# A fused mLSTM and two mixture-of-experts layers: the first w_in conversion placed behind the first score products, and a last routing with a split position

## The chip, the cores and the metric

One core of a Trainium2 chip runs the kernel. The metric is the device time of one execution in microseconds (us); lower is better. Times of instructions come from one profiled execution of the kernel before, counted from its first instruction.

## The reference

```python
# 1. mLSTM: batch 2, 8 heads, 768 steps, head width 40
m_new = max(f[t] + m, i[t]); C = exp(f[t]+m-m_new) * C + exp(i[t]-m_new) * outer(v[t], k[t])   # n likewise with k[t]
y[t] = sigmoid(o[t]) * (C @ q[t]) / max(abs(n @ q[t]), 1)
# 2. x: 1536 tokens x 320
g = softplus(x @ w_in);  x = g @ w_out                       # inner width 2048
# 3. 8 experts, each token goes to one
e = argmax(x @ w_gate)
out = softmax(x @ w_gate)[e] * sigmoid(x @ w_output_gate)[e] * (relu(x @ w1[e]) @ w2[e])   # inner width 1024
```

## The kernel before, in words

The mLSTM runs in chunks of 128 steps (NCH = 6) for two batches b. For each chunk and batch the gates are scanned (`gates`), a mask and the decays are made (`mask`, `decay`, ScalarE exponentials), the scores `sp` are multiplied on TensorE for the two halves hh of the heads and weighted by the decays on VectorE (`scores`; the result replaces the decays in tile `abc`), `pv` multiplies them with the values, and the result x goes to the first feed-forward layer. Chunk c of both batches is block c of 256 tokens.

Precision is kept by splitting every fp32 operand into a rounded fp32r part and its rest, so that products are made in several passes. `conv` (line 796) does that for the 16 pieces n of w_in and w_out, which arrive as 64-bit numbers: three VectorE operations each turn the two words into fp32 (`to_f32`, tiles `wra` and `wta`), a copy rounds, and two subtractions, on VectorE (`low`) and GpSimd (`low_p`), make the rest. The raw buffers are three; the load of the fourth piece on the SP queue waits until the first is read. `up1` and `down1` are the products `ph` and `acc` of this layer, for all blocks.

After the last f of a block, `route` finds each token's expert and its place in the expert's slots of 128 rows, and GpSimd scatters the rows to DRAM. For the last block `place_last` (line 1054) does the placing: from the counts per expert (`tot`), the rank of a token among those of its expert (`rank`), the room left in the expert's open slot (`room`), its next free row (`nxt`) and the new slots opened (scan `cum`), with `base` the correction for tokens that go to a new slot. The slots 0 to 3 don't wait for the scatter: `early_turn` transposes the rows that are in DRAM already (`er`) into `xe` and adds the last block's rows by products with a selection matrix `S` (1 where a row's place equals the column's number), for the rounded parts first and the rests (`parts_of`, `have_lows`) second; `early_x` splits `xe` into `flat` and its rest. Then `second` runs the experts in four quarters: `up` (`ph`), transposes `tp`, `down` (`yp`). Slots from 4 on load their rows (`yac`) after the scatter and transpose them as `xslot`.

The order on every engine is made by a planner on the host, the class `Weaver` (line 46). Tasks are generators; each says which events it waits for and on which engine its next operation goes. The planner keeps a modelled clock for each engine and gives the next place to the task that could start earliest; where two could start at the same time, the one with the lower rank goes first, and then the one added first. After an operation its task can't start the next dependent one on the same engine at once (0.13 us in the model), so others come in between. `W.op("P", cost)` adds modelled time on TensorE. On the chip each engine runs its list in order, and semaphores hold what isn't ready.

`warm(event, n)` puts n bf16 products of 512 columns, which nobody reads, on TensorE when `event` is marked. In the last routing: `known` is marked when the expert numbers of the first slots are read into TensorE's registers (`get_experts`), `have_turned` when the twelve transposes of `early_turn` are placed, `turned_rows[0]` when the first row group of the last block is transposed, and `have_last_lg` when its logits are done.

Of the kernel before, what the change touches and what calls it, by code (L numbers as in the profile page):

```python
# [14 lines left out]
ALU = mybir.AluOpType  # L15
# [219 lines left out]
def mlstm_moe_kernel(ctx: ExitStack, tc: tile.TileContext, q_t, k_t, k, v, i_gate, f_gate, o_gate,  # L235
# [142 lines left out]

    scored_1 = Event(n=2 * B - 1)
# [168 lines left out]
    def chunk(b, c):  # L548
# [65 lines left out]
        def scores(hh):  # L614
            yield [have_kt[b][c], have_q[c], masked[hh]]
            half = box["dd"][:, :, hh]
            sp, ev = yield from bank.get([P, NP, P], F32, "sp")
            for n in range(NP):
                if n % 2 == 0:
                    yield "P"  # L620
                PE.matmul(sp[:, n, :], kT[0:104, hh, n, :], qT[0:104, n, :], start=True, stop=True)
            W.signal(used_kt[b][c])
            W.signal(used_q[c])
            if c == 1:
                W.signal(scored_1)
            yield [decayed[hh]]
            yield "V"
            DVE.tensor_tensor(out=half, in0=sp, in1=half, op=ALU.mult)
            W.signal(ev)
            W.signal(scored[hh])  # L630
# [165 lines left out]
    def conv():  # L796
        for n in range(NF):
            W.cur.rank = RANKS[n]
            yield [have_raw[n]] + ([have_g[0]] if n == 0 else [])
# [72 lines left out]
    def tt(out_, a, b_, op):  # L872
        DVE.tensor_tensor(out=out_, in0=a, in1=b_, op=op)
# [180 lines left out]
    def place_last(small, tot, rank, ohb, ef, ssum, row, row_ev, ev, counts_ev, small_ev, blk, whole):  # L1054
# [5 lines left out]
        dn, t8, c1, c2 = (small[:, o9 + n * E:o9 + (n + 1) * E] for n in range(4))  # L1060
        own = small[:, 0:2]
# [4 lines left out]
        tt(m, rank, over(room, T2), ALU.is_ge)  # L1066
        yield "V"
        DVE.tensor_tensor_scan(out=cum, data0=newp, data1=more_p, initial=0.0, op0=ALU.add, op1=ALU.add)
        tt(nr, rank, over(nxt, T2), ALU.add)
        yield "V"  # L1070
        DVE.scalar_tensor_tensor(out=dn, in0=u, scalar=float(P), in1=base, op0=ALU.mult, op1=ALU.subtract)
        yield "V"
        tt(m, m, over(dn, T2), ALU.mult)
        yield "V"
        tt(nr, nr, m, ALU.add)
        yield "V"
        tt(nr, nr, ohb, ALU.mult)
# [3 lines left out]
        DVE.tensor_copy(out=posi, in_=pos)  # L1081
# [4 lines left out]
        for t in range(T2):  # L1086
            yield "V"
            DVE.tensor_scalar(out=chosen["S"][:, t], in0=chosen["iota"], scalar1=pos[:, t:t + 1], scalar2=None,
                              op0=ALU.is_equal)
# [375 lines left out]
    W.add(gates(1, 1, 2), 0.5)  # L1465
# [21 lines left out]
    def get_experts(s0, s1, ready, when):  # L1487
# [16 lines left out]
        W.op("P", 0.35 + 0.1 * (s1 - s0))  # L1504
# [18 lines left out]
    W.add(warm(known, 3), 0)  # L1523
    W.add(warm(turned_rows[0], 2), 0)
    W.add(warm(have_last_lg, 2), 0)
# [295 lines left out]
```

## Time and profile before

| | |
|---|---|
| median of three runs | 428.53 us (427.74 to 428.86) |
| the profiled execution | 425.7 us, its span 423.9 us |
| busy in the span: TensorE, VectorE, ScalarE, GpSimd | 97%, 78%, 71%, 45% |
| mean granted TensorE clock | 0.988 of full |
| data moved | 62.9 MB, mean 148 GB/s |

The span runs from the first to the last instruction; the execution's own time has 1.8 us more around it. Busy time of TensorE is modelled from the starts of its products, and a product that follows another closely is counted with its pipeline time. The idle time given in brackets behind a row is the time for which its engine had nothing to do before it, and behind the arrow stands what ended that. A row that says x12 stands for twelve instructions in a row, its second number is the time that they cover.

### The profile page before, as it was taken

The page shows a single profiled execution, that of the slowest core. Times are in us where ns is not written, and L with a number is a line of the kernel's source. Part 1 is how long each engine was busy: PE and PEld are TensorE (multiplying, and loading weights), DVE is VectorE, ACT ScalarE, POOL GpSimd, SP SyncE. Part 2 cuts the span into 40 slices and gives each one's busy share as a digit, 9 for nine tenths or more (in the row PEclk, how much of TensorE's full clock was granted, in tenths as well). Part 3 has the DMA queues.
Part 4 walks back from the last instruction along what each step waited for, and adds up shares of the span by engine and source line. Part 5 has one row for each costly group of instructions (what it writes and reads, how often), then busy time and mean ns, then how long its engine had stood idle before and what let it go on. Part 6 is the DMA issues. An engine that isn't in the chain of part 4 may idle for free.

```text
span 423.9 us, 9886 instructions
## 1 busy us (share of the span) xinstructions
PE 409.6 (97%) x3095; PEld 390.7 (92%) x3095; DVE 330.6 (78%) x900; ACT 301.2 (71%) x880; POOL 189.6 (45%) x256
## 2 busy tenths in 40 slices
PE   8898999999999999999999999989999999999994
PEld 7787999999989999999999999878999999999993
DVE  4997999889988999998765756756853686697863
ACT  3677999979767877876867877656788774675421
POOL 5265665656041102221210102127666867777765
PEclk9999999999999999999999999979999999999998
DMA  8959597581218982212100101128735836835022
GB/s 264 340 179 316 189 295 225 178 212 54 77 63 281 337 275 67 64 50 76 39 18 22 40 2 38 39 101 264 249 96 166 249 132 194 247 125 178 12 88 93
DMA packets 32283, 62.89 MB, mean 148 GB/s; under 512 B 4218, under 2 KB 16765, under 8 KB 32230
## 3 DMA queue, kind: packets, MB, share of 16 engines
q1 hardware_dynamic: 30742, 57.87, 43.6%
q0 software_dynamic: 1488, 4.35, 2.8%
q8 instruction: 28, 0.46, 0.4%
q14 instruction: 25, 0.20, 0.2%
HBM read 54.05 MB, written 8.65 MB: 148 GB/s over the span
## 4 chain that ended last, share of the span: by engine, by line
PE 87%; DVE 5%; ACT 3%; DMA 2%; POOL 1%; issue 1%; SPq 1%; POOLq 0%; ACTq 0%
PE ph L196 34%; PE acc L196 20%; PE yp L196 13%; PE pv L196 5%; PE sp L196 4%; PE tp L196 3%; PE lg L196 2%; DMA wra<-in_w_in_dram 2%; PE qc L196 2%; PE xe L196 1%; PE kv L196 1%; PE x2tp L196 1%; DVE wta L196 1%; PE xp L196 1%; SPq L196 1%
## 5 line engine op out<-in xcount | busy, mean ns | idle before, releaser
L196 ACT ACTIVATE ab<-ab 128x256 f32<-128x256 f32 x192 | 77.3, 415 | 2.6
L196 PE MATMUL ph<-w1s,flat 128*128 x312 | 60.9, 332 | 0.5 <-ACT flat L196 0.4
L196 POOL TENSOR_TENSOR w1s<-w1raw,w1s 64x256 fp32r<-64x256 f32 (+1 forms) x39 | 40.9, 1062 | 36.7 <-ACT w1s L196 16.2
L196 PE MATMUL acc<-win,gh 128*128 128x320 f32 x240 | 55.4, 316 | 0.4 <-ACT gh L196 0.4
L196 PE MATMUL yp<-w2s,hh 128*128 x240 | 54.6, 315 | 0.0
L196 PEld LDWEIGHTS ph<-w1s,flat 128*128 128x128 f32 x312 | 46.5, 189 | 5.0 <-ACT flat L196 0.6
L196 POOL TENSOR_TENSOR w2s<-w2raw,w2s 128x640 fp32r<-128x640 f32 x30 | 46.9, 1593 | 8.5 <-issue 5.0
L196 DVE SCALAR_TENSOR_TENSOR g<-ph,ab 128x256 f32<-128x256 f32 x96 | 40.0, 420 | 13.7 <-ACT ab L196 12.7
L196 ACT ACTIVATE ab<-ph 128x256 f32<-128x256 f32 x96 | 36.4, 379 | 18.0 <-PE ph L196 17.2
L196 DVE TENSOR_TENSOR gl<-g,gh 128x256 fp32r<-128x256 f32 x96 | 41.8, 442 | 8.5 <-ACT gh L196 7.9
L196 DVE TENSOR_TENSOR hr<-ph,hr 128x256 f32<-128x256 f32 x60 | 25.3, 424 | 27.2 <-ACT hr L196 27.0
L196 POOL DMA_INDIRECT rows<-row,rsm x12 | 12.5, 1044 | 75.1 <-DVE nxt L196 29.7
L196 ACT CAST gh<-g 128x256 fp32r<-128x256 f32 x94 | 37.3, 398 | 9.5 <-DVE g L196 9.0
L196 ACT COPY hr<-ph 128x256 f32<-128x256 f32 x60 | 23.0, 383 | 28.2 <-PE ph L196 28.2
L196 PE MATMUL ph<-win 128*128 128x256 f32 x250 | 41.4, 287 | 0.0
L196 PEld LDWEIGHTS yp<-w2s,hh 128*128 128x128 f32 x240 | 39.8, 188 | 1.5 <-issue 0.6
L196 PEld LDWEIGHTS acc<-win,gh 128*128 128x128 f32 x240 | 38.6, 189 | 1.0 <-ACT gh L196 0.9
L196 PE MATMUL yp<-w2s,hl 128*128 x120 | 37.2, 310 | 0.0
L196 PE MATMUL acc<-win,gl 128*128 128x320 f32 x120 | 37.2, 310 | 0.0
L196 PEld LDWEIGHTS ph<-win 128*128 128x128 f32 x250 | 34.5, 190 | 0.0
L196 PE MATMUL acc<-wou,gh 128*128 128x320 f32 x144 | 33.4, 316 | 0.0
L196 ACT CAST w2s<-w2raw 128x640 fp32r<-128x640 f32 x32 | 23.2, 745 | 14.0 <-PE yp L196 14.0
(211 smaller groups left out, 1065.5 us busy)
## 6 DMA issues: line engine op xcount, KB each, us to landing
w1raw<-in_w_dram SPq DMA_DIRECT2D x32, 384.0 KB, 3.1
wra<-in_w_in_dram SPq DMA_DIRECT2D x16, 704.0 KB, 6.9
w2raw<-in_w_dram SPq DMA_DIRECT2D x32, 320.0 KB, 3.4
abc<-abc_dram SPq DMA_DIRECT2D x4, 1024.0 KB
rows<-pad SPq DMA_DIRECT2D x19, 194.0 KB, 5.9
qT<-in_q_t_dram SPq DMA_DIRECT2D x6, 512.0 KB, 3.9
kn<-in_k_dram SPq DMA_DIRECT2D x5, 416.0 KB, 7.4
vn<-in_v_dram SPq DMA_DIRECT2D x6, 320.0 KB, 5.2
```

What stands on the lines that cost most here:

```text
L196: return fn(*args, **kw)
```

## The change

Four edits. `conv` waits, for its first piece, until two of the four weighted scores of chunk 0 are placed (event `scored_0`), instead of the first chunk's gates. The task of chunk 1's gates has rank 1.1 instead of 0.5, behind the conversion (rank 1 for the first four pieces). `place_last` computes the place of a token as two numbers, `pos` (row in the open slots, with the correction) and `new` (128 times the number of slots opened before the expert's), which are added for the scatter; the selection matrix subtracts the first and compares with the second in one operation. The planner counts reading the expert numbers with 0.1 us, where it counted 0.35 and 0.1 for each slot; the three warm-ups behind it wait for `have_turned`, those behind the first transposed rows are one instead of two, and those behind the last logits four instead of two.

```diff
+    scored_0 = Event(n=2)
     scored_1 = Event(n=2 * B - 1)
...
             W.signal(ev)
+            if c == 0:
+                W.signal(scored_0)
             W.signal(scored[hh])
...
-            yield [have_raw[n]] + ([have_g[0]] if n == 0 else [])
+            yield [have_raw[n]] + ([scored_0] if n == 0 else [])
...
-        dn, t8, c1, c2 = (small[:, o9 + n * E:o9 + (n + 1) * E] for n in range(4))
-        own = small[:, 0:2]
+        c1 = small[:, o9 + 2 * E:o9 + 3 * E]
+        own, new = small[:, 0:2], small[:, 3 * T2:4 * T2]
+        far = small[:, o8 + 2 * T8:o8 + 3 * T8].rearrange("p (t e) -> p t e", e=E)
...
         tt(m, rank, over(room, T2), ALU.is_ge)
+        tt(nr, rank, over(nxt, T2), ALU.add)
         yield "V"
         DVE.tensor_tensor_scan(out=cum, data0=newp, data1=more_p, initial=0.0, op0=ALU.add, op1=ALU.add)
-        tt(nr, rank, over(nxt, T2), ALU.add)
-        yield "V"
-        DVE.scalar_tensor_tensor(out=dn, in0=u, scalar=float(P), in1=base, op0=ALU.mult, op1=ALU.subtract)
-        yield "V"
-        tt(m, m, over(dn, T2), ALU.mult)
-        yield "V"
-        tt(nr, nr, m, ALU.add)
-        yield "V"
+        DVE.scalar_tensor_tensor(out=m, in0=m, scalar=float(P), in1=ohb, op0=ALU.mult, op1=ALU.mult)
         tt(nr, nr, ohb, ALU.mult)
         yield "V"
+        DVE.scalar_tensor_tensor(out=far, in0=m, scalar=1.0 / P, in1=over(base, T2), op0=ALU.mult, op1=ALU.mult)
+        tt(m, m, over(u, T2), ALU.mult)
+        yield "V"
+        tt(nr, nr, far, ALU.subtract)
+        DVE.tensor_reduce(out=new, in_=m, axis=AX.X, op=ALU.add)
+        yield "V"
         DVE.tensor_reduce(out=pos, in_=nr, axis=AX.X, op=ALU.add)
         yield "V"
-        DVE.tensor_copy(out=posi, in_=pos)
+        tt(posi, pos, new, ALU.add)
...
-            DVE.tensor_scalar(out=chosen["S"][:, t], in0=chosen["iota"], scalar1=pos[:, t:t + 1], scalar2=None,
-                              op0=ALU.is_equal)
+            DVE.tensor_scalar(out=chosen["S"][:, t], in0=chosen["iota"], scalar1=pos[:, t:t + 1],
+                              scalar2=new[:, t:t + 1], op0=ALU.subtract, op1=ALU.is_equal)
...
-    W.add(gates(1, 1, 2), 0.5)
+    W.add(gates(1, 1, 2), 1.1)
...
-        W.op("P", 0.35 + 0.1 * (s1 - s0))
+        W.op("P", 0.1)
...
-    W.add(warm(known, 3), 0)
-    W.add(warm(turned_rows[0], 2), 0)
-    W.add(warm(have_last_lg, 2), 0)
+    W.add(warm(have_turned, 3), 0)
+    W.add(warm(turned_rows[0], 1), 0)
+    W.add(warm(have_last_lg, 4), 0)
```

## Rows read from the trace of the kernel before

**Rows 1.** The page's 40 slices: the granted TensorE clock in tenths.

```profile
PEclk9999999999999999999999999979999999999998
```

**Rows 2.** Busy time of each engine by stage; first the stretch and its length.

```profile
13.80:36.00 22.20, 19.62 (x174) 17.91 (x175) 21.47 (x46) 15.06 (x54) 9.19 (x13) 1.00 0.80 247
36.00:45.00 9.00, 7.86 (x58) 6.20 (x57) 6.53 (x15) 7.75 (x23) 6.18 (x10) 1.00 1.02 326
45.00:275.30 230.30, 229.24 (x1831) 226.05 (x1830) 195.41 (x581) 181.69 (x563) 67.14 (x108) 1.00 0.38 118
...
288.45:417.60 129.15, 128.65 (x876) 120.86 (x873) 91.21 (x201) 82.28 (x197) 92.24 (x97) 1.00 0.53 168
```

**Rows 3.** Timeline of VectorE at the start: start, time covered, instructions, idle before.

```profile
11.80 1.04 DVE L196 TENSOR_SCALAR wta<-wra 128x704 uint32<-128x704 uint32 x1 [0.43 <-DMA wra<-in_w_in_dram]
...
13.70 1.27 DVE L196 TENSOR_TENSOR abc<-sp,abc 128x512 f32<-128x512 f32 x2
...
19.34 0.16 DVE L196 TENSOR_SCALAR gts<-gps 128x16 f32<-128x16 f32 x1
```

**Rows 4.** VectorE's busy time on tile scratch (chunk 1's gate split).

```profile
11.80:18.00 6.20, 1.36 (x5) 1.00 1.03 345
```

**Rows 5.** Timelines of ScalarE and TensorE at the start.

```profile
11.38 0.20 ACT L196 COPY sm<-abc 128x4 f32<-128x4 f32 x1
...
15.12 1.95 PE L196 MATMUL pv<-v,abc 128*128 128x123 f32 x16 [1.34 <-DVE abc L196]
```

**Rows 6.** Timelines of the SP queue and GpSimd: chunk 2's cumulated gates.

```profile
27.83 0.33 SPq L196 DMA_DIRECT2D abc_dram<-acum  x1
31.23 0.39 SPq L196 DMA_DIRECT2D abc<-abc_dram  x1
...
39.37 1.60 POOL L196 TENSOR_SCALAR_AFFINE_SELECT abc<-abc 128x512 f32<-128x512 f32 x2 [0.40 <-DMA abc<-abc_dram]
```

**Rows 7.** Timeline of TensorE around the last routing.

```profile
278.46 0.59 PE L196 MATMUL warm<-ones 128*128 128x512 bf16 x2
...
279.71 0.17 PE L196 MATMUL counts<-rsm,tri 128*128 128x8 bf16 x1 [0.66 <-DVE rsm L196]
...
279.84 2.24 PE L196 MATMUL xe<-ident,er 128*128 128x128 f32 x12
...
282.49 5.32 PE L196 MATMUL xe<-S,part 128*128 128x256 f32 x20 [0.42 <-DVE S L196]
...
287.66 0.82 PE L196 MATMUL warm<-ones 128*128 128x512 bf16 x3
...
288.45 4.00 PE L196 MATMUL ph<-w1s,flat 128*128 x24
```

**Rows 8.** Busy time in 1 us stretches; the third number from the end is the clock.

```profile
280.00:281.00 1.00, 1.00 (x8) 1.00 (x8) 0.95 (x10) 1.00 (x6) 0.00 (x0) 0.73 0.00 0
287.00:288.00 1.00, 1.00 (x7) 0.73 (x6) 0.76 (x3) 0.79 (x4) 1.00 (x2) 0.85 0.00 0
```

**Rows 9.** Timeline of VectorE in the last placing: first, third last, second last, selection.

```profile
280.02 0.17 DVE L196 TENSOR_TENSOR newp<-counts,room 128x8 f32<-128x8 f32 x1
...
281.59 0.17 DVE L196 TENSOR_REDUCE rsm<-rsm 128x2 f32<-128x16 f32 x1
...
281.79 0.17 DVE L196 CAST rsm<-rsm 128x2 uint32<-128x2 f32 x1
281.87 0.88 DVE L196 TENSOR_SCALAR S<-iota,rsm 128x512 fp32r<-128x512 f32 x2
```

**Rows 10.** Timeline of the other engines behind the selection.

```profile
280.55 3.85 ACT L196 CAST w2s<-w2raw 128x640 fp32r<-128x640 f32 x6
...
284.37 0.97 POOL L196 DMA_INDIRECT rows<-row,rsm  x1 [0.30 <-issue]
...
287.14 1.61 DVE L196 TENSOR_TENSOR flat<-xe,flat 128x256 fp32r<-128x256 f32 x4 [2.85 <-ACT flat L196]
287.29 2.35 SPq L196 DMA_DIRECT2D yac<-rows  x5
```

More of the change, by code (lines that the diff above doesn't have):

```diff
@@ L1066, in place_last @@
         tt(m, rank, over(room, T2), ALU.is_ge)
+        tt(nr, rank, over(nxt, T2), ALU.add)
         yield "V"
         DVE.tensor_tensor_scan(out=cum, data0=newp, data1=more_p, initial=0.0, op0=ALU.add, op1=ALU.add)
-        tt(nr, rank, over(nxt, T2), ALU.add)
+        DVE.scalar_tensor_tensor(out=m, in0=m, scalar=float(P), in1=ohb, op0=ALU.mult, op1=ALU.mult)
+        tt(nr, nr, ohb, ALU.mult)
         yield "V"
-        DVE.scalar_tensor_tensor(out=dn, in0=u, scalar=float(P), in1=base, op0=ALU.mult, op1=ALU.subtract)
+        DVE.scalar_tensor_tensor(out=far, in0=m, scalar=1.0 / P, in1=over(base, T2), op0=ALU.mult, op1=ALU.mult)
+        tt(m, m, over(u, T2), ALU.mult)
         yield "V"
-        tt(m, m, over(dn, T2), ALU.mult)
-        yield "V"
-        tt(nr, nr, m, ALU.add)
-        yield "V"
-        tt(nr, nr, ohb, ALU.mult)
+        tt(nr, nr, far, ALU.subtract)
+        DVE.tensor_reduce(out=new, in_=m, axis=AX.X, op=ALU.add)
         yield "V"
```

## The prediction, made before the result was known

> **What bounds the kernel now.** I read the page's slices first, then the busy time by stage, then timelines of the two stages that the diff touches. TensorE bounds most of it: from 45.0 to 275.3 us it is idle for only 1.06 of 230.3 us, and from 288.45 to 417.6 for 0.5 of 129 us [rows 2]. In between there is nearly nothing to win, and whatever brings TensorE's work forward at either end of these stretches is carried to the end of the span. The slack is in two places. At the start, TensorE is idle for 2.58 us between 13.8 and 36 and for 1.14 us between 36 and 45 [rows 2], while VectorE has 0.73 us of idle in the 22.2 us of the first of these stretches: VectorE is the engine that is late there. At the last routing the granted clock drops, the one 7 in the middle of the page's clock row [rows 1].
>
> All times below are of the profiled execution, 425.7 us with a span of 423.9. The three plain runs have a median of 428.53, 2.8 more; I work out differences in the profile and apply them to 428.53. A measurement tells 0.3%, 1.29 us, from no change.
>
> **Part 1, the start.** Before, VectorE stops for 0.43 us until the first w_in piece lands, runs that piece's first conversion step at 11.80 (1.04 us), a step of chunk 1's gates, and the second conversion step, and comes to chunk 0's first two score products only at 13.70 [rows 3]. What these need was there earlier: the last ScalarE step of both decays ends at 11.58 [rows 5]. TensorE waits 1.34 us for the second of them and starts pv at 15.12, so it was free at 13.78 [rows 5]. With the change no conversion can be placed ahead of the two products. They take 1.27 us [rows 3]; from 11.37 (the end of VectorE's work before its 0.43 us of waiting) they end at 12.64, or, if the five operations that split chunk 1's cumulated gates (1.36 in sum [rows 4]) all go first, at 14.0. Both are within 0.25 us of 13.78, so the wait of 1.34 us shrinks to 0 to 0.25.
>
> What of these 1.1 to 1.3 us lasts? VectorE's work up to 36 us is the same, only in another order, and it is full but for 0.73 us. So the lasting gain has VectorE's recovered idle time as its near bound, 0.4, and the whole TensorE wait as its far one, 1.3. The conversion itself ends later: three steps, put behind two products, end 0.4 to 1.3 us after where they did. Queued behind the third step are SP's next w_in load (it needs the raw buffer) and, behind that load on SP, chunk 1's second k, v and k-natural loads. DMA is at 80% of its engines over this stretch [rows 2], so those loads sit in a backlog anyway, and I cost the shift at nothing; without that backlog it would cost up to 1.3 us at chunk 1's v. Chunk 1's remaining gate steps yield to the conversion where both are ready; that loss is rival (c). I take **0.6 us gained**, nearer to the recovered idle time since the work is conserved, with 1.3 gained and 1.9 lost as ends.
>
> **Part 2, the last routing's chain.** From the first compare at 280.02 to the first selection product S at 281.87 it is 1.85 us [rows 9]. A step that needs the one just before costs 0.20 us (the reduction at 281.59 to the cast at 281.79); one that doesn't costs 0.08 (that cast to S, which doesn't read it) [rows 9]. Before, eight dependent stages with eleven operations; after, six stages with thirteen, S reading two per-partition scalars. Two stages less at 0.20 is 0.40; two operations more at 0.08 each fill the gaps of the others, and the three operations of the gate weight, which now stand between the stages and cost stalls of their own, fit into the same gaps. I take **0.45 us**, bounds 0.1 and 0.6; the scatter's position comes earlier by the same. S takes about 0.4 us per token group [rows 9]; a second scalar might slow it, by at most the 0.1 us that the low bound allows for.
>
> **Part 3, warm-up products and clock.** TensorE's order around the routing is: logits, two warm-ups (278.46), nothing for 0.66 us until the counts at 279.71, twelve transposes xe from 279.84, a wait for S, twenty products xe from 282.49 (5.32 us), three warm-ups from 287.66, two small ones, and the first expert products ph at 288.45 [rows 7]. The granted clock is full up to 280, 0.73 in the mean of 280 to 281, and 0.85 in that of 287 to 288 [rows 8], so at 1.2 instead of 2.4 GHz from about 280.5 to 287.3: all twenty xe products ran at half speed. In units of 256 columns they are 24 (eight single and two double ones, twice), 0.222 us each. The 24 ph products behind them are 32 units in 4.00 us with their drain [rows 7], 0.12 each. At full clock xe takes 2.9 us instead of 5.32.
>
> The change puts two more warm-ups behind the logits (at 278.46, where 0.66 us are idle; the two take 0.59 us by their row, so two more nearly fill the gap and delay nothing), takes one away behind the first transposed rows, and moves three from behind xe to between the transposes and xe, since the planner no longer counts 1.15 us (0.35, and 0.1 for each of eight slots) for reading the experts' numbers. So the stretch before the drop gets 0.4 us more of dense products. That this holds the clock is not shown by any row: what the row shows is that two warm-ups, small products and transposes did not.
>
> The rows say that TensorE was busy with transposes just as the clock fell. The Trainium skill (TensorE: Matmul & The Clock Gate, Part 4: PE-mode transpose) says that transposes don't count as a busy TensorE for the clock as other products do. The trace agrees: the clock fell in the middle of twelve transposes in a row. By that rule the dense products in front and behind decide; if transposes counted, the added warm-ups would change less, and the time would be that of rival (a), 428.1 instead of 425.9.
>
> If the clock holds: S 0.45 earlier lets xe start at 282.0; the first half ends at 283.45, the low parts (two subtractions on VectorE behind S, about as long as the two S, 0.9) are there at 283.3, and the second half ends at 284.95. The conversion of xe is then late next: ScalarE is on its w2 casts until 284.40 [rows 10]; a first xe cast takes about 0.4, as a subtraction of the same width does (four take 1.61 [rows 10]), and three subtractions end at 286.0. So ph starts at 286.0 instead of 288.45: 2.45 us. Behind it, the rows of the later slots leave at 287.29 [rows 10], and come only 0.45 earlier; four slots of ph (about 3.8 us) stand in front of their first use, which covers it. In a plain run the half-speed stretch need not lie as here, so I take **2.0 us** for parts 2 and 3 together, bounds 1.2 and 2.6.
>
> Sum: 0.6 + 2.0 = 2.6; 428.5 - 2.6 = **425.9**, with 424.3 to 427.4 as this case's own range.
>
> **The rivals.** (a) *The clock falls as before.* Then the transposes still end at 282.08, and the three moved warm-ups at half speed (two units, 0.44 each) end at 283.4, ahead of xe: xe starts 0.9 late, ends at 288.7, and nothing but the two small products stands behind it; ph starts 0.2 later than before. With the start's 0.6: 428.53 - 0.4 = 428.1. For it: behind the first transposed rows stands one warm-up less. Against it: 1.0 us of warm-ups instead of 0.6 close before the drop.
>
> (b) *The gain is held up behind xe.* If ScalarE's order puts more w2 casts (six in 3.85 us, 0.64 each [rows 10]) ahead of the xe casts, or the slots' rows are waited for, only about 0.9 of the 2.0 stays: 428.53 - 1.5 = 427.0. For it: the rows come only 0.45 earlier. Against: the four slots of cover.
>
> (c) *Slower: chunk 1's gates come late.* The last gate step of chunk 1, at 19.34 [rows 3], releases the gates of chunks 2 to 5, whose sums are stored at 27.83 and loaded back at 31.23; GpSimd's mask of chunk 2 waits for that load (0.40 us, 39.37) [rows 6], and TensorE is short of work there [rows 2]. If two more conversion steps (1.04 each) and the two products (1.27) all go ahead of the gates, that is 3.3 us. The store has some 1.4 us to spare: 3.4 us to the load, less about 2 for landing, as from a scatter's end at 285.34 to the load that waits for it at 287.29 [rows 10]. So it decides from 1.4 us on; 3.3 makes chunk 2 1.9 us late, with no gain in front: 428.53 + 1.9 = 430.4 where the clock falls too. Against it: the gates' steps are short, and fit into the 0.1 us gaps between dependent conversion steps, whatever their rank.
>
> **How the numbers follow.** Forecast 0.50, (a) 0.22, (b) 0.16, (c) 0.12. Predicted is the likeliest, 425.9. The range 424.0 to 429.0 takes in the forecast, (a) and (b), and leaves out (c) and a tail of the forecast with the largest terms, together under 0.2. Faster by over 1.29 us, below 427.2: nearly all of the forecast, two thirds of (b), a little of (a), 0.61. Within: 0.27. Slower: most of (c) and a tail of (a), 0.12.
>
> **What would show it.** Right: score products of chunk 0 right behind 11.4, pv at about 13.9; a granted clock of 1.00 through 280 to 288; xe in about 3 us; ph at about 286. Part 1 is wrong if pv still starts near 15, or if TensorE has regained as much idle time by 45 us as it lost at 13.8. Part 3 is wrong if the clock falls anyway, which is the largest single risk, or if ph starts at 288 in spite of a full clock.

## The result: 0.8% slower, and where it shows in the profile

The changed kernel takes 432.91 us (430.00 to 434.69), the kernel before, run beside it, 429.91 (427.74 to 430.95): a ratio of 1.0079, 95% interval 1.0064 to 1.0094. Forecast was 425.9 with a range of 424.0 to 429.0, so both the sign and the range are wrong.

The profiled execution of the changed kernel has a span of 431.5 us, 7.6 more than the one before. Cut at five events of TensorE's timeline, the difference lies here:

| from, to | before | after | more |
|---|---|---|---|
| start of the span to the first score product `sp` | 9.05 | 10.21 | 1.16 |
| to the last block's first transpose `x2tp` | 266.41 | 267.63 | 1.22 |
| to slot 4's first product `ph` | 18.48 | 18.61 | 0.13 |
| to the start of the last product | 123.34 | 125.59 | 2.25 |
| to the end of the span | 6.58 | 9.43 | 2.85 |

Not all of this is the change. The first line is the moment at which the clock first rises to 2.4 GHz (3.99 us before, 6.94 after), which sets how fast the opening products run; it lies between 3.96 and 7.17 us in the twenty profiles of this case, in kernels of both kinds. The last line is a wait at the end that did not come again in a second profile of the same kernel (below). What is left for the change in this profile is 1.2 us up to the last block, nothing at the routing, and 2.25 us behind it, where the clock falls once more (297.07 to 300.48 us); a second profile of the same kernel doesn't have that late fall.

The clock by slices (answers [rows 1]): the 7 in the middle is gone, an 8 has come in the third slice, and one behind the routing.

```profile
PEclk9989999999999999999999999998999999999997
```

Busy time by stage, in order TensorE, its weight loads, VectorE, ScalarE, GpSimd, then the clock (answers [rows 2]): the first stretch now has a mean clock of 0.92, and VectorE is idle in it for 2.44 us where it was for 0.73; the second is emptier (TensorE 7.35 of 9.00 us, 7.86 before), and the last has 3.2 us of idle where it had 0.5.

```profile
13.80:36.00 22.20, 19.60 (x163) 18.06 (x162) 19.76 (x41) 14.63 (x53) 9.67 (x12) 0.92 0.66 213
36.00:45.00 9.00, 7.35 (x59) 6.07 (x57) 6.98 (x14) 7.11 (x21) 5.35 (x8) 1.00 1.03 323
45.00:277.84 232.84, 231.56 (x1851) 228.87 (x1851) 198.49 (x588) 185.39 (x571) 68.62 (x109) 1.00 0.38 120
288.24:422.40 134.16, 130.97 (x876) 122.58 (x873) 91.86 (x203) 83.98 (x200) 94.48 (x99) 0.99 0.52 162
```

The start on VectorE (answers [rows 3]). The first two products `abc` stand ahead of the conversion, as intended; but all three conversion steps `wta` now stand between them and the second two, where before only the third did. The last line, of an operation that waits for the second `pv`, shows that the slower TensorE holds VectorE up in turn.

```profile
14.08 1.29 DVE L196 TENSOR_TENSOR abc<-sp,abc 128x512 f32<-128x512 f32 x2
15.40 0.28 DVE L196 TENSOR_TENSOR scratch<-scratch 16x128 bf16<-16x128 f32 x1
15.72 1.01 DVE L196 TENSOR_SCALAR wta<-wra 128x704 uint32<-128x704 uint32 x1
16.76 1.82 DVE L196 SCALAR_TENSOR_TENSOR wta<-wra,wta 128x704 uint32<-128x704 uint32 x2
18.50 0.16 DVE L196 TENSOR_SCALAR sm<-pv 128x8 f32<-128x8 f32 x1
18.57 0.68 DVE L196 TENSOR_TENSOR abc<-sp,abc 128x512 f32<-128x512 f32 x1
...
19.24 0.68 DVE L196 TENSOR_TENSOR abc<-sp,abc 128x512 f32<-128x512 f32 x1
...
23.24 0.17 DVE L196 TENSOR_SCALAR sm<-pv 128x8 f32<-128x8 f32 x1 [1.53 <-PE pv L196]
```

Before, between the two pairs:

```profile
15.26 0.88 DVE L196 SCALAR_TENSOR_TENSOR wta<-wra,wta 128x704 uint32<-128x704 uint32 x1
...
16.64 0.69 DVE L196 TENSOR_TENSOR abc<-sp,abc 128x512 f32<-128x512 f32 x1
```

TensorE there (answers [rows 5]). The wait at the first `pv` fell from 1.34 to 0.58 us. A new one of 1.16 stands behind `kv`, where TensorE waited for nothing before, and the second `pv` takes 3.13 us instead of 1.95.

```profile
15.52 1.95 PE L196 MATMUL pv<-v,abc 128*128 128x123 f32 x16 [0.58 <-DVE abc L196]
17.30 0.94 PE L196 MATMUL kv<-v,kn 128*104 128x82 f32 x8
19.40 0.20 PE L196 MATMUL gps<-ident,acum 16*128 16x16 f32 x1 [1.16 <-DVE sm L196]
...
20.07 3.13 PE L196 MATMUL pv<-v,abc 128*128 128x123 f32 x16 [0.18 <-DVE sm L196]
```

The second `pv` takes longer because the clock stands at half from 20.59 to 24.00 us (the first line below). At the routing it is full, in the stretches that answer to [rows 8] too (the second line).

```profile
21.00:22.00 1.00, 1.00 (x6) 1.00 (x6) 0.71 (x2) 0.97 (x3) 0.21 (x1) 0.50 1.02 420
...
287.00:288.00 1.00, 1.00 (x9) 0.92 (x8) 0.00 (x0) 0.64 (x3) 0.70 (x1) 1.00 0.45 171
```

The routing on TensorE (answers [rows 7]): the twenty `xe` products take 3.40 us instead of 5.32, and `ph` starts 10.40 us behind `x2tp` instead of 12.99. Then the transposes `xslot` wait twice for the loaded rows, and slot 4's products (the `ph` at 296.45) come 18.61 us behind `x2tp`, as late as before (18.48).

```profile
284.87 3.40 PE L196 MATMUL xe<-S,part 128*128 128x256 f32 x20 [0.50 <-DVE S L196]
...
288.24 4.20 PE L196 MATMUL ph<-w1s,flat 128*128 x24
292.27 0.60 PE L196 MATMUL tp<-ident,hr 128*128 128x128 f32 x4
293.28 0.55 PE L196 MATMUL xslot<-ident,yac 128*128 128x128 f32 x3 [0.41 <-DMA yac<-rows]
295.16 0.55 PE L196 MATMUL xslot<-ident,yac 128*128 128x128 f32 x3 [1.33 <-DMA yac<-rows]
296.45 1.57 PE L196 MATMUL ph<-w1s,flat 128*128 x6 [0.74 <-ACT flat L196]
```

Before, the same transposes found their rows there:

```profile
292.73 0.82 PE L196 MATMUL xslot<-ident,yac 128*128 128x128 f32 x6
293.94 1.37 PE L196 MATMUL ph<-w1s,flat 128*128 x6 [0.40 <-ACT flat L196]
```

VectorE's placing, from the first compare to the selection (answers [rows 9]): 1.79 us instead of 1.85.

```profile
282.39 0.17 DVE L196 TENSOR_TENSOR newp<-counts,room 128x8 f32<-128x8 f32 x1
...
284.10 0.16 DVE L196 TENSOR_TENSOR rsm<-rsm 128x2 uint32<-128x2 f32 x1
284.18 0.99 DVE L196 TENSOR_SCALAR S<-iota,rsm 128x512 fp32r<-128x512 f32 x2
```

GpSimd's two scatters (answers [rows 10]): the first takes 1.88 us, where it took 1.25 at 282.81 before, and the second starts 2.19 us behind it instead of 1.56.

```profile
285.11 1.88 POOL L196 DMA_INDIRECT rows<-row,rsm  x1 [9.09 <-ACT w2s L196]
287.30 0.98 POOL L196 DMA_INDIRECT rows<-row,rsm  x1 [0.30 <-issue]
```

### The profile page after: what moved, and what is told of

It reads as the page before. It is cut to its first block, busy times and chain, and to the rows that moved or that the text cites. A ratio compares the mean times of both kernels' runs of the same rounds, so it can differ in the third digit from the quotient of the medians.

```text
span 431.5 us, 9875 instructions
## 1 busy us (share of the span) xinstructions
PE 411.3 (95%) x3096; PEld 392.7 (91%) x3096; DVE 331.5 (77%) x902; ACT 303.4 (70%) x880; POOL 191.7 (44%) x256
## 4 chain that ended last, share of the span: by engine, by line
PE 81%; DVE 5%; issue 4%; ACT 3%; DMA 3%; POOL 3%; POOLq 0%; SPq 0%; ACTq 0%; DVEq 0%
PE ph L196 31%; PE acc L196 19%; PE yp L196 11%; PE pv L196 4%; PE sp L196 4%; PE tp L196 3%; PE heat L196 2%; PE lg L196 2%; PE qc L196 1%; POOL out_dram L196 1%; DMA og<-in_o_gate_dram 1%; ACT y L196 1%; DMA yac<-rows 1%; DVE wta L196 1%; PE xslot L196 1%
## 5 line engine op out<-in xcount | busy, mean ns | idle before, releaser
L196 PE MATMUL ph<-w1s,flat 128*128 x312 | 62.0, 336 | 0.8 <-ACT flat L196 0.7
L196 DVE TENSOR_TENSOR gl<-g,gh 128x256 fp32r<-128x256 f32 x96 | 43.7, 458 | 11.4 <-ACT gh L196 10.8
L196 PEld LDWEIGHTS ph<-w1s,flat 128*128 128x128 f32 x312 | 47.7, 192 | 5.2 <-ACT flat L196 1.0
```

The source lines that it names most:

```text
L196: return fn(*args, **kw)
```

## The experiments

All ratios are to the kernel before, run on the same chip beside them; intervals are of 95%. Kernels that stand in one table ran on different chips in part, so it is their ratios that compare, not their times. The theories have letters:

- S: the two start edits carry the loss. S1: they do so because the conversion steps ahead of the second pair open a wait and the clock falls. S2: they do so because chunk 1's gates come later.
- C: what the start edits cost is the clock. O: it is the new order itself.
- H: the routing's gain is lost in the wait for the loaded rows.
- T: the wait at the end belongs to the changed kernel.
- P: the selection with two numbers slows the scatter.

**Which edits cost.** The two start edits together (start_only) and each by itself; behind each line stands the run that has it, the new event's own line is left out:

```diff
+            if c == 0:                                                     # scored_only, start_only
+                W.signal(scored_0)
-            yield [have_raw[n]] + ([have_g[0]] if n == 0 else [])          # scored_only, start_only
+            yield [have_raw[n]] + ([scored_0] if n == 0 else [])           # scored_only, start_only
-    W.add(gates(1, 1, 2), 0.5)                                             # rank_only, start_only
+    W.add(gates(1, 1, 2), 1.1)                                             # rank_only, start_only
```

place_only is the new `place_last`, warm_only the planner's cost and the three groups of warm-ups, rest both of these, a_again the changed kernel once more.

> Before, with only the two edits of the start: the conversion behind the first two score products, and chunk 1's gates at rank 1.1. Theory S: 1 to 3 us slower, with the first ph 1.3 us or more later, counted from the first score product. Theories T and H: within 0.5 us of before.

> The kernel before with the first start edit alone: the first w_in conversion waits until two of chunk 0's weighted scores are placed; chunk 1's gates keep rank 0.5. Theory S1 (all three conversion steps come to stand ahead of chunk 0's second pair of weighted scores, TensorE waits about 1.1 us for it at 18 to 19.4, and the clock falls behind that wait in most executions): as both start edits together, ratio 1.003 to 1.007. Theory S2 (the later gates of chunk 1 cost, whatever the conversion does): 0.999 to 1.001.

> The kernel before with the second start edit alone: chunk 1's gates at rank 1.1 instead of 0.5. Theory S1: the first conversion steps stay where they were, TensorE waits 1.3 us at pv as before and none at 18 to 19.4; ratio 0.999 to 1.001. Theory S2: 1.003 to 1.007.

> Before, with only the new arithmetic of the last placing. TensorE's program has as many instructions as before. Theories T and S: within 0.4 us of before. Theory H: the selection comes at most 0.1 us earlier (in the change it did, seen from the counts), so within 0.4 us as well, unless the scatter behind it takes longer as in the change (1.88 us instead of 1.25 for its first half), then up to 0.6 slower.

> Before, with only the warm-up products and the planner's cost for reading the expert numbers as in the change. Theory T (tail): the change has one TensorE product and its weight load more than before, which moves the end of TensorE's program against the 16 KB pieces in which it is loaded, and the last branch waits about 3 us for its target; here that pair is there too, so 1.5 to 2.5 us slower than before, with a gap of 2.5 to 3 us between TensorE's last branch and its next instruction. Theory H (hand-off): the granted clock holds through the routing and ph starts some 2.5 us earlier, but the rows of slots 4 and later are not there, so 0 to 1 us slower, no gap at the end. Theory S (start): the loss is all in the reordered start, so 0 to 2 us faster here.

> The changed kernel without its two start edits (the split position and the moved warm-ups alone). Theory S: what is left is the sum of the two alone (1.001 and 1.0013), ratio 0.999 to 1.003, mean clock 0.995 or above. Rival (the parts disturb each other, or the loss lies at the routing and the end): 1.004 to 1.008.

> The changed kernel once more, beside the others, for a second profile and for its granted clock. Theory S (the two start edits carry most of the loss, by a clock that falls once more in most executions): ratio 1.006 to 1.009, a mean clock of 0.985 to 0.990 where the kernel before has 0.995, and half speed in the profile within 3 us behind the wait at 19. Theory T (the 3.0 us without an instruction behind TensorE's last branch belongs to this kernel): the gap of about 3 us is there again; if it belonged to that execution, it is 0.4 us and the end behind the last product is as short as before (about 6.6 us).

| kernel | median us | before | ratio |
|---|---|---|---|
| start_only | 427.74 | 425.59 | 1.0048 [1.0019, 1.0078] |
| scored_only | 426.96 | 425.34 | 1.0054 [1.0031, 1.0076] |
| rank_only | 428.37 | 425.34 | 1.0055 [1.0025, 1.0084] |
| place_only | 425.92 | 425.59 | 1.0010 [0.9995, 1.0026] |
| warm_only | 425.62 | 425.59 | 1.0013 [0.9991, 1.0036] |
| rest | 426.38 | 425.51 | 1.0018 [0.9993, 1.0043] |
| a_again | 427.95 | 425.51 | 1.0047 [1.0020, 1.0073] |

The start edits carry the loss; the other two parts give nothing. That each start edit costs as much as both was expected by neither theory: S1 and S2 each had one of them at no cost. The rank alone moves one gate step (`gts`, [rows 3]) from 19.34 to 23.13 us and opens waits of 0.20 and 0.76 us at 18.8 and 20.1; the event alone opens the wait of 1.19 us between `kv` and `gps`. Both open waits where TensorE is thinly loaded. Of rank_only:

```profile
20.06 2.95 PE L196 MATMUL pv<-v,abc 128*128 128x123 f32 x16 [0.76 <-DVE sm L196]
```

Of scored_only:

```profile
18.56 0.20 PE L196 MATMUL gps<-ident,acum 16*128 16x16 f32 x1 [1.19 <-DVE sm L196]
```

In a_again's profile the five cuts of the table above differ from before by 1.10, 1.11, -0.65, 0.58 and 0.09 us: the start is as late as in the first profile, the routing gives 0.65 and what follows takes it back.

**The conversion behind all four products.** The event counts four instead of two.

```diff
-    scored_0 = Event(n=2)
+    scored_0 = Event(n=4)
```

> Both start edits, but the conversion waits for all four weighted scores of chunk 0 instead of two. Theory S1: no conversion step stands ahead of the second pair, so the wait of 1.1 us at 18 to 19.4 is gone while the wait at the first pv stays as short as with the edits (0.6 to 0.8 instead of 1.34); ratio 0.997 to 1.000. Rival: the first piece of w_in is converted some 2 us later and the first expert-free products ph (36 us) come late by that, ratio 1.003 to 1.006.

428.91 us, 1.0090 [1.0067, 1.0114]. The wait at 18 us is gone, as S1 said, but waits of 1.51 and 1.36 us stand at 24.5 and 28.4 instead, the clock falls from 30.51 to 37.33, and the first layer's first `ph` comes at 42.03 instead of 35.50, 5.5 us later counted from the first `sp`. So S1's cure failed; the rival has the direction, but its 2 us at `ph` and its range, 1.003 to 1.006, are too small.

**Is it the clock?** The granted clock's records show where it stood at 1.2 GHz, ahead of the last product:

| start as | kernel: first rise; falls (us) |
|---|---|
| before | before 3.99: 280.47-287.29; place_only 4.23: 280.71-284.12; rest 7.03: 280.10-283.51; place_one 3.96: 294.10-297.51; none in warm_only 5.14, before_warm2 6.63, warm_rows 4.14, warm_cover 5.65 |
| edited | after 6.94: 20.59-24.00, 297.07-300.48; a_again 6.83: 20.48-23.89; a_heat43 6.25: 19.91-23.32, 296.38-299.80; rank_only 7.14: 20.79-24.21; start4 6.61: 30.51-37.33; start_warm 5.17: 46.13-49.54; after_warm 7.17: 27.66-31.07; start_only 4.98: 281.46-284.87; scored_only 4.32: none |
| edited, products at five waits | start_warm2 6.28: 282.76-286.17; rank_warm2 5.05: 281.53-284.95; after_warm2 6.15: none |

No profile with the old start falls before 280 us (0 of 8); with the edited start 7 of 9 do, the two with the earliest first rise (4.32 and 4.98 us) don't. The moment of that rise differs between the two groups too; of the profiles of the first two rows in which it comes behind 6 us, the six with the edited start all fall early, the two with the old one (rest, before_warm2) don't.

The timed runs have a mean clock each, which doesn't say where the clock fell. It is 0.995 or more in 92 of 124 runs of the kernel before on the four chips of these comparisons, in 1 of 8 of start_only, 3 of 8 of scored_only, 2 of 12 of rank_only, 3 of 12 of a_again. In the edited kernels the time goes with it: rank_only's two such runs took 423.10 and 423.84 us, its others 426.72 to 429.31; a_again's three have a median of 425.81, its others 428.13; start_only's one took 424.96, its others have a median of 427.93. In the kernel before the runs below 0.995 take only 0.3 to 1.3 us more in the median than its others on the same chip.

To change the clock and nothing else, bf16 products that nobody reads were put into TensorE's waits, at no cost in the planner, so that every engine keeps its order: four behind the first `kv` (start_warm, after_warm), or 13 to 19 at five places (start_warm2, after_warm2, rank_warm2, and before_warm2 as the control).

```diff
+            if c == 0 and b == 0:
+                W.mark(first_kv)
...
+        kept = W.clock["P"], dict(W.columns), W.tick, W.hot
+        for _ in range(extra):
+            PE.matmul(t, ones, ones.unsqueeze(1).to_broadcast([P, 4, P]), start=True, stop=True)
+        W.clock["P"], W.columns, W.tick, W.hot = kept
...
+    W.add(warm(first_kv, 0, extra=4), 0)
```

> Both start edits, and four bf16 products that nobody reads put on TensorE behind the first kv products, into the wait of 1.1 us at 18 to 19.4; they are free in the planner, so that the order of the rest stays as with the start edits alone (those gave 427.7 us, 1.0048 [1.0019, 1.0078]). Theory S1 with the clock as the cost: the granted clock is 1.00 over 19 to 24 in the profile, and the ratio falls to 1.000 to 1.002. If instead the order of VectorE's work costs and not the clock, the ratio stays at 1.004 to 1.006.

> The changed kernel with four more bf16 products that nobody reads behind the first kv products, in TensorE's wait at 18 to 19.4; free in the planner. Theory S with the clock as the larger part: as start_warm against start_only, the mean clock rises by 0.004 or more against the changed kernel and the time falls by 1 to 2 us, ratio 1.003 to 1.005. If the clock were not the cause: as the changed kernel, 1.006 to 1.009.

> Both start edits and 19 products more that nobody reads, at the five places between 13 and 46 us where TensorE waits (3 behind the last scores of chunk 0, 4 behind the first kv, 3 behind qc of chunk 1, 4 and 5 behind the two groups of warm-ups at 38 and 42); free in the planner, so that every engine keeps its order of the start edits. The start edits alone gave 1.0048 at a mean clock of 0.990, with the four behind kv 1.0036 at 0.995. Theory C (what the start edits cost is the clock): mean clock 0.997 or more and a ratio of 0.999 to 1.0015. Theory O (the order itself costs about 1 us, by new waits for ScalarE and VectorE at 18 and 43 us): mean clock as high, and still 1.002 to 1.004.

> The kernel before with 13 such products at the same five places (3, 2, 3, 3, 2), and its own order on every engine: the control for the two kernels beside it. Theory C: its clock hardly falls at the start in most executions, so that the gain is small, ratio 0.997 to 1.000. The same from theory O. Above 1.001 the extra products themselves would cost time.

> The edit of the rank alone (1.0055; its executions at a mean clock of 0.995 and above took 423.1 and 423.8 us, those at 0.988 some 428.4) and 14 such products at the five places (3, 3, 1, 1, 6). Theory C: nearly all executions like the two quick ones, ratio 0.995 to 0.999. Theory O: 1.002 to 1.005.

> The changed kernel with the 19 further warm-up products of start_warm2, free in the planner, so that every engine keeps the changed kernel's order. Theory C (the loss is the clock at the start; the split position and the moved warm-ups alone gave 1.0018): ratio 1.000 to 1.003. If the changed kernel lost elsewhere as well: 1.0045 to 1.008, as without these products.

| start | without | 4 products | 13 to 19 products |
|---|---|---|---|
| before | 1 | | 1.0008 [0.9991, 1.0025] |
| both edits | 1.0048 [1.0019, 1.0078] | 1.0036 [1.0019, 1.0052] | 1.0005 [0.9986, 1.0025] |
| changed kernel | 1.0079 [1.0064, 1.0094], 1.0047 [1.0020, 1.0073] | 1.0038 [1.0015, 1.0061] | 1.0013 [0.9996, 1.0030] |
| rank alone | 1.0055 [1.0025, 1.0084] | | 1.0034 [1.0014, 1.0053] |

The four products alone give little back: 1.0036 instead of 1.0048, in neither theory's range, and for the changed kernel 1.0038 beside a_again's 1.0047 on the same chip, which the intervals don't tell apart. Thirteen to nineteen products that compute nothing take the edited start back to the control's time (425.49 us beside 425.64) and the changed kernel to within 0.13% of the kernel before, and they don't help where the start is the old one. The list of instructions of every engine is otherwise the same, so the clock is the likely way by which they help; together with the plain runs above it speaks for theory C as the larger part, for both edits together. In start_warm2 the clock is full where it had fallen in the changed kernel:

```profile
20.00:22.00 2.00, 2.00 (x19) 1.97 (x20) 1.77 (x5) 1.83 (x8) 0.10 (x1) 1.00 1.04 347
22.00:24.00 2.00, 2.00 (x23) 1.75 (x22) 1.95 (x4) 1.43 (x4) 0.83 (x1) 1.00 0.76 301
```

Four things don't fit. In start_warm the clock is as good as in the kernel before beside it (0.996 and 0.995 in the median), and it is still 0.36% slower. The mean clock of start_warm2 is 0.994 in the median, not the 0.997 that C expected; in its profile (0.993) all of the half speed lies at the routing and behind the last product. Its profile, one execution at 427.05 us, has `x2tp` at 278.40, 2.1 us behind the control's 276.29, without a fall before it: the order's own waits (for the mask of chunk 2 on GpSimd, for `gh` on ScalarE) are still there, and where the timed runs win them back no profile shows. The other profiles agree with this one: from the first `sp` to the last block's `x2tp` the eight with the old start take 266.06 to 266.81 us, and the twelve with an edited one 267.30 to 270.35, whether the clock falls in between (267.50 to 268.83, start4's 270.35 apart) or not (267.30 to 268.51, five profiles, three of them with the products). So up to there the new order costs some 1.5 us in the mean without any fall, as theory O says. But start_only and scored_only win that back at the routing, where slot 4 comes 16.97 and 16.49 us behind `x2tp` instead of 18.48; their profiled executions, which have no fall before 280 us, took 425.41 and 425.52, as long as the kernel before in the median (425.59 and 425.34). And for the rank alone half of the loss stays with the products. That the start edits carry the loss is shown; how it splits between clock and order is not.

**Chunk 2's gates.** The forecast's rival (c) can be read without a run of its own: chunk 2's sums are loaded at 33.92 and its mask starts at 42.38 (answers [rows 6]), 3.0 us later than before, of which 1.16 is the later start of everything.

```profile
33.92 0.39 SPq L196 DMA_DIRECT2D abc<-abc_dram  x1
...
42.38 1.25 POOL L196 TENSOR_SCALAR_AFFINE_SELECT abc<-abc 128x512 f32<-128x512 f32 x2 [0.58 <-DMA abc<-abc_dram]
```

With the rank alone, which is the rival's own edit and gave 1.0055, the mask is as late (1.25 of it the later start), behind a longer wait for that load:

```profile
42.37 1.87 POOL L196 TENSOR_SCALAR_AFFINE_SELECT abc<-abc 128x512 f32<-128x512 f32 x2 [1.05 <-DMA abc<-abc_dram]
```

**Where the routing's gain goes.** In warm_only the clock holds, `xe` takes 3.34 us and `ph` starts 10.34 us behind `x2tp`; slot 4 still starts 18.09 behind it, for slot 5's rows are waited for ahead of slot 4's products:

```profile
290.57 0.49 PE L196 MATMUL xslot<-ident,yac 128*128 128x128 f32 x3
292.55 0.55 PE L196 MATMUL xslot<-ident,yac 128*128 128x128 f32 x3 [1.49 <-DMA yac<-rows]
293.84 1.20 PE L196 MATMUL ph<-w1s,flat 128*128 x6 [0.74 <-ACT flat L196]
```

before_warm2 has the old warm-ups and, in its profile, no fall; it too meets rows that are only just there:

```profile
287.29 4.00 PE L196 MATMUL ph<-w1s,flat 128*128 x24
...
291.92 1.06 PE L196 MATMUL xslot<-ident,yac 128*128 128x128 f32 x6 [0.18 <-DMA yac<-rows]
```

Both keep warm_only's edits. warm_rows takes the rows out of TensorE's way, so that its experts compute something else for these slots; warm_cover puts slot 5's transposes behind slot 4's products (the line that takes them away from their old place is left out).

```diff
-            PE.transpose(xp[:, kk, :], row[:, kk * P:(kk + 1) * P], ident)         # warm_rows
+            PE.transpose(xp[:, kk, :], ident, ident)
...
-                        for s_ in (6, 7):                                          # warm_cover
+                        for s_ in (5, 6, 7):
```

> The kernel before with the moved warm-ups alone, and the transposes xslot of the slots from 4 on read the identity matrix instead of the loaded rows, so that TensorE doesn't wait for these rows; with that the experts compute something else for these slots, and the work is the same. Theory H (the gain of the held clock is lost in the wait for these rows): slot 4's first product comes 15.8 to 16.6 us behind the last block's first transpose x2tp (18.1 with the moved warm-ups, 18.5 before) and the time falls by 1.5 to 2.3 us against the moved warm-ups alone, ratio 0.995 to 0.998. Rival (other work holds it up as well: the split of xslot, the w2 casts): 17.5 us or more, ratio 0.999 to 1.002.

> The kernel before with the moved warm-ups, and the transposes xslot of slot 5 put behind slot 4's first products, ahead of those of slots 6 and 7: slot 4's rows land some 2 us before slot 5's, and its products then don't stand behind the wait for the latter. Theory H (the held clock's gain is lost in the wait for the loaded rows): slot 4's first product 16.4 to 17.2 us behind the last block's x2tp (18.1 with the moved warm-ups alone, 16.0 without any wait for rows), ratio 0.996 to 0.999, faster than both kernels. Rival: the wait only moves to slot 5's products, ratio 0.999 to 1.002.

warm_rows: 424.04 us, 0.9968 [0.9949, 0.9987], slot 4 at 291.47, 16.04 us behind `x2tp`. That is 0.32% less than the kernel before, and 0.45% less than warm_only's ratio, as theory H said. The kernel before without these rows was not run; its profile shows no wait for them.

```profile
290.26 0.82 PE L196 MATMUL xslot<-ident 128*128 128x128 f32 x6
291.47 1.37 PE L196 MATMUL ph<-w1s,flat 128*128 x6 [0.40 <-ACT flat L196]
```

warm_cover: 428.77 us, 0.9998 [0.9980, 1.0015]. Slot 4 comes 16.04 us behind `x2tp`, earlier than H expected, but slot 8 is only 0.94 us ahead of warm_only's and the last product 0.11: rows are waited for again, and a `yp` later on waits 0.6 us for VectorE, as in the changed kernel's profile and not in warm_only's. So the wait only moved, as the rival expected with 0.999 to 1.002; whether the wait for VectorE took some of the gain as well isn't settled. No version with the reference's computation beat the kernel before.

```profile
292.22 1.37 PE L196 MATMUL ph<-w1s,flat 128*128 x6 [0.73 <-ACT flat L196]
293.42 0.49 PE L196 MATMUL xslot<-ident,yac 128*128 128x128 f32 x3
294.18 0.88 PE L196 MATMUL xslot<-ident,yac 128*128 128x128 f32 x6 [0.27 <-DMA yac<-rows]
```

**The later second scatter.** All other profiles with the split position have 2.17 to 2.19 us between the starts of the scatters, those without it 1.55 to 1.57. place_one keeps the split and adds the parts before the selection.

```diff
-        tt(posi, pos, new, ALU.add)
+        tt(pos, pos, new, ALU.add)
+        yield "V"
+        DVE.tensor_copy(out=posi, in_=pos)
...
-                              scalar2=new[:, t:t + 1], op0=ALU.subtract, op1=ALU.is_equal)
+                              scalar2=None, op0=ALU.is_equal)
```

> The split position alone, but its two parts are added before the selection matrix, which compares with one number as in the kernel before (one dependent step more). In the runs with the split position the second scatter of rows starts 2.18 us behind the first, without it 1.56. Theory P (the selection with two numbers per partition slows the first scatter beside it): 1.56 again, and the selection takes 0.88 instead of 1.00 us. Rival (the shorter chain puts the scatter beside other VectorE work): 2.18 stays. Time within 0.999 to 1.002 either way.

1.56 us again, and `S` 0.88, the numbers of theory P. But the edit changes a second thing: the scatter's row numbers are made by a copy again, as in the kernel before, and not by an addition. And the selection hardly stands beside the scatter: in the changed kernel `S` ends at 285.17, 0.06 us behind the scatter's start. So the two operations together make the scatter 0.6 us longer; which of them does isn't shown. The time is the same, 1.0017 [0.9994, 1.0041].

```profile
282.57 1.25 POOL L196 DMA_INDIRECT rows<-row,rsm  x1 [9.30 <-DVE S L196]
284.13 0.97 POOL L196 DMA_INDIRECT rows<-row,rsm  x1 [0.30 <-ACT w2s L196]
```

**The wait at the end.** In the profile of the changed kernel VectorE's last two sums wait 3.03 us behind the last product:

```profile
425.00 1.01 DVE L196 SCALAR_TENSOR_TENSOR yac<-yp,cc,yac 128x320 f32<-128x320 f32 x2 [3.03 <-remote]
```

a_heat43 issues one opening product less, to shift the code.

```diff
-HEAT = 44
+HEAT = 43
```

> The changed kernel with 43 instead of 44 start-up products, so that TensorE's program is as long as before; the order of everything else is that of the change. Theory T: 1.5 to 2.5 us faster than the change, 0.5 to 1.5 us slower than before, and no gap behind TensorE's last branch. Theories H and S: as the change, 3 us slower than before.

428.45 us, 1.0058 [1.0032, 1.0083], without the wait. But a_again, the same code as the changed kernel, hasn't got it either:

```profile
419.77 0.55 DVE L196 SCALAR_TENSOR_TENSOR yac<-yp,cc,yac 128x320 f32<-128x320 f32 x1 [0.33 <-PE yp L196]
```

It is in both profiles of the last comparison, after_warm2 (2.34 us) and warm_cover (2.31), where the kernel before took 428.88 us instead of the 425.1 to 425.6 of the other comparisons. So theory T falls: the wait isn't the changed kernel's. That the kernel before pays it too where it takes 429 us fits (its profiled execution, 425.7, is 2.8 below its plain runs and has no such wait), but no profile of it there shows it.

## Why the prediction was wrong

**Part 1: the step that failed.** The first wait shrank, by 0.76 instead of 1.1 to 1.3: four of the five gate operations went first, near the later of the two cases. (Some of the 0.76 is the later start: with the old start and as late a rise of the clock, rest has 0.83 at this place. In scored_only, which starts 0.33 us later than before, the wait is 0.54.) The loss came from products that the text never followed: chunk 0's second pair. "VectorE's work up to 36 us is the same, only in another order" is right, and for this very reason the conversion steps that left the first pair's way stood in the second's; the wait of 1.34 at `pv` became 0.58 there and 1.16 behind `kv`. The text listed what queues behind the conversion (loads, gates) and not what TensorE asks VectorE for next, so "I cost the shift at nothing" is the term that failed: with the conversion's edit alone it is 0.54% lost. The recovered idle time of VectorE, the near bound of the gain, didn't come either: its idle between 13.8 and 36 us grew from 0.73 to 2.44 us. The lasting sum was 0.6 gained; measured is 2.15 us lost for the start edits (425.59 to 427.74).

**The clock at the start: the rival that was missing.** Part 3 weighed warm-ups at the routing, and the text didn't ask whether the start's clock hung on its order. The rows had the stretch at a full clock, but with 2.58 us of idle [rows 1, 2]; the same kind of waits, moved within it, now go with a fall in most profiles. The Trainium skill (TensorE: Matmul & The Clock Gate, A second HAM failure mode: psum-queue depth-cycling) tells of a clock that goes up and down where TensorE idles briefly but often between groups of products that cycle through the banks of PSUM. The trace agrees as far as the brief waits go: ahead of the fall at 20.59 us stand waits of 0.58, 1.16 and 0.18 us. That the banks of PSUM have a part in it no run here shows.

**Part 2.** 0.45 us was forecast, 0.06 measured, below the low bound of 0.1. Fewer stages don't help where the gate weight's operations stand in the same list and stall between them, and the sum for the scatter has the wrong sign for its second half, which starts 0.55 us later behind the counts (5.21 us instead of 4.66). The bound of 0.1 us for the selection's second number was right for the selection itself (0.99 instead of 0.88), and missed GpSimd's scatter.

**Part 3.** The first half of the mechanism came true: the clock holds through the routing, `xe` takes 3.40 us (2.9 forecast), `ph` comes 2.6 us earlier behind `x2tp` (2.45 forecast). That the moved warm-ups hold it is likely, not shown: of nine profiles with them one falls between 280 and 288 us, of eleven without them five. But the 2.0 us are not there. The step that failed is "four slots of ph (about 3.8 us) stand in front of their first use, which covers it": the four slots (4.0 us) cover the rows only while `ph` itself is late; 2.6 us earlier, TensorE stands at rows that land when they did. That was rival (b), with 0.9 us left; measured is nothing left. And the price was taken from an execution that isn't the usual one on four of the five chips with a record of it: a fall of 6.82 us over 424 lowers the mean clock by 0.008, and 92 of 124 runs there have a mean clock of 0.995 or more, so no such fall. (On the fifth, that of after_warm2 and warm_cover, 4 of 23 have, where the longer end can lower the mean too. For the kernel before in the first comparison it isn't on record.)

**The rivals.** (a) was wrong where it was weighed, at the routing. (c) was right in kind: chunk 1's last gate step comes 2.2 us later than before, 1.16 of it the later start, and chunk 2's mask some 1.8 without that start, near the 1.9 that the rival has. Its own edit, the rank alone, cost 0.55%; the two runs of it with a mean clock of 0.995 or more don't show that loss, so the late mask isn't the whole of it. It had 0.12, and the right sign.

## What to carry to other kernels

When an operation is moved behind another on an engine that is full, follow the next few things that the slower engine asks of it, not only the one that gets served sooner: the wait moves one place on. Where TensorE is thinly loaded, its clock can be part of the price of a reordering; a few unread products in the waits, free in the plan so that nothing else moves, and the mean clocks of the plain runs are two ways to ask, and a profile of the same stretch without a fall is the third. Here they didn't agree in full. A gain ahead of a load is worth only as much as the load's own slack, and a price read from one execution should be held against the mean clocks of the plain runs first.

## What the runs showed of the hardware

The clock first rises anywhere between 3.96 and 7.17 us in executions of nearly the same opening, and the places of later falls shift with it (20.59 us behind a rise at 6.94, 19.91 behind one at 6.25), so one profile shows one of several outcomes. It falls without any long wait: the longest one ahead of 20.59 us is 1.16 us. With the split position GpSimd's first scatter takes 1.87 or 1.88 us in seven profiles, with the position of the kernel before, or with its selection and copy (place_one), 1.25 or 1.26 in thirteen. In three of twenty profiles, of three kernels, the last sums wait 2.3 to 3.0 us behind the last product; the two of them that were taken side by side come from a chip where the kernel before is 3.4 us longer too.
